# Opening loads, repeated weight rows and last PSUM tiles of a parallel attention and ReLU block

## Chip, cores and metric

The kernel runs on one core of a Trainium2 chip. Its time is device time in microseconds. Three runs of the kernel before gave 1164.60 to 1164.73, median 1164.63.

## The reference

```python
x: (1, 2048, 576); wqkv: (576, 1728); wo: (576, 576); w1: (576, 4608); w2: (4608, 576)   # all float32
xn  = layernorm(x)
# A: 32 heads of 18; each token attends to itself and to 7 earlier ones, 2 apart
q, k, v = heads(xn @ wqkv)
logits  = (q . k[pos - 2*w]) * 18 ** -0.5          # w = 0..7, masked where pos - 2*w < 0
a       = (softmax(logits) . v[pos - 2*w]) @ wo
# B: a dense block
b       = relu(xn @ w1) @ w2
return x + a + b
```

## The kernel before

The 2048 tokens are worked on in two phases (even and odd tokens) of 8 token tiles of 128 each; two token tiles make a block of 256 columns. Every matmul operand is split into a high part (rounded to fp32r) and a low part (the rest), and a product is the sum of high x high, low x high and high x low. 576 is four times 128 and 64 left over; the 64 remaining rows of a weight are kept twice, in the lower and the upper half of the 128 partitions, so that one matmul does two of the terms of the remainder.

The main loop runs over 288 steps `n` (phase, 12 chunks of 3 x 128 columns of w1, 4 blocks of tokens, 3 columns f). In a step TensorE does the 14 matmuls of `h_mm(n + 2)` (xn @ w1 into a PSUM tile `ph`), then the 12 of `o_mm(n)` (relu(h) @ w2 into PSUM tiles `po`, one for each of the two token tiles, accumulated over f). After f = 2, `o_out` adds the two `po` tiles to the token tiles in SBUF (VectorE, L606), which frees them for the next block. ScalarE takes ReLU of `ph` as `hhi` (L556), VectorE makes `hlo` (L559). `ph`, `po` and `pm` have two buffers each; a `po` takes two PSUM banks, a `ph` or `pm` one, so all eight banks are used. Attention, its projections (`qkv_tile`, `wo_a` to `wo_b`) and the next phase's normalisation are put between these steps at step numbers written in tables; VectorE's part of attention is dealt out by `run_bg` so that it keeps pace with TensorE.

Weights come through a list of tasks ordered by step. A task has a load into one of five staging tiles `st` and a split: `two()` makes the high part on ScalarE (L145) and the low part on VectorE (L149), or on GpSimd (L147) for a few steps. Loads are issued three tasks ahead of the splits by `stage_more`, all on SP's DMA queue, in order; each waits until its staging tile is free. `w1_task` loads a tile in one transfer for the 512 full rows and two for the 64 remaining ones (L157, L161, L162); `wo_tasks` loads five tiles, the fifth (kt = 4) being the 64 remaining rows, again in two transfers (L212, L213). The fifth wo tile is split at steps 119 and 263; f is 2 there.

The opening is written out by hand from L682 on. It loads the first two token tiles in halves on SP's and ACT's queue (`load_x`, L236), then w1 and w2 tiles and further token tiles on SP. The first tile is normalised by ScalarE, the second by VectorE, both are transposed by TensorE and split (`make_xt`), and then the first h matmuls start. At the end the last step adds the two halves of the columns of each token tile apart (L612) and stores them on both queues (L615, L617).

Of the kernel before, what the change touches and what calls it, by code (L numbers as in the profile page):

```python
# [10 lines left out]
F32 = mybir.dt.float32  # L11
F32R = mybir.dt.float32r
AF = mybir.ActivationFunctionType
# [4 lines left out]
P = 128  # L18
NPH = 2
NI = 8  # L20
# [5 lines left out]
C = 3  # L26
# [12 lines left out]
HEADW = (-9, -8, -7, -6, -5, -4)  # L39
# [16 lines left out]
def tile_body(ctx: ExitStack, tc: tile.TileContext, x, wqkv, wo, w1, w2, out):  # L56
    nc = tc.nc
    S, D = x.shape
# [5 lines left out]
    KT = 4  # L64
    DR = D - KT * P
    D2 = D // 2
    CUT = (slice(0, 256), slice(256, D))
# [22 lines left out]
    ps_o = pool("ps_o", 2, space=PSUM)  # L90
    ps_h = pool("ps_h", 2, space=PSUM)
    ps_m = pool("ps_m", 2, space=PSUM)
# [10 lines left out]
    for _ in range(WARM):  # L103
        nc.tensor.transpose(warm[:, 0, 0:P], ident, ident)

    x_v = x.rearrange("(p i two) d -> two i p d", i=NI, two=NPH)
    o_v = out.rearrange("(p i two) d -> two i p d", i=NI, two=NPH)


    t = {"pe": 0.0, "dve": 0.0}  # L110

    def mm(o, l, r, start, stop, n):
        nc.tensor.matmul(o, l, r, start=start, stop=stop)  # L113
        t["pe"] += n / 2400.0 + 0.002

    def dve(n):
        t["dve"] += (n + 130) / 960.0
# [6 lines left out]
    def split_task(step, load, split):  # L124
        tasks.append((step, load, split))

    def stage_more(ahead=AHEAD):
        while tasks and len(staged) < ahead:
            step, load, split = tasks.popleft()
            st = stp.tile([P, 640], F32, name="st")  # L130
            load(st)
            staged.append((step, split, st))
# [9 lines left out]
    step_now = None  # L142

    def two(hi, lo, src, n):
        nc.scalar.activation(hi, src, AF.Copy)  # L145
        if step_now in by_pool:
            nc.gpsimd.tensor_tensor(lo, src, f32(hi), op=ALU.subtract)  # L147
        else:
            nc.vector.tensor_tensor(lo, src, f32(hi), op=ALU.subtract)  # L149
            dve(n)  # L150

    W1, W2, WQ, WO = {}, {}, {}, {}

    def w1_task(step, key, f):
        def load(st):
            c = slice(f * P, (f + 1) * P)
            nc.sync.dma_start(  # L157
                st[:, 0:512].rearrange("p (k c) -> p k c", k=KT),
                w1[0 : KT * P, c].rearrange("(k p) c -> p k c", p=P),
            )  # L160
            nc.sync.dma_start(st[0:DR, 512:640], w1[KT * P : D, c])  # L161
            nc.sync.dma_start(st[DR:P, 512:640], w1[KT * P : D, c])  # L162

        def split(st):
            w = w1p.tile([P, 2, 5 * P], F32R, name="w1t")
            two(w[:, 0, :], w[:, 1, :], st[:, :], 640)
            W1[key] = w

        split_task(step, load, split)
# [36 lines left out]
    def wo_tasks(steps, key):  # L206
        def one(kt):
            def load(st):
                if kt < KT:
                    nc.sync.dma_start(st[:, 0:D], wo[kt * P : (kt + 1) * P, :])  # L210
                else:
                    nc.sync.dma_start(st[0:DR, 0:D], wo[KT * P : D, :])  # L212
                    nc.sync.dma_start(st[DR:P, 0:D], wo[KT * P : D, :])  # L213

            def split(st):
                if kt == 0:
                    a = wqp.tile([P, 7, D], F32R, name="wq")
                    b = vp.tile([P, 3, D], F32R, name="v")
                    WO[key] = [a[:, k, :] for k in range(7)] + [b[:, k, :] for k in range(3)]
                w = WO[key]  # L220
                two(w[kt], w[5 + kt], st[:, 0:D], D)

            return load, split

        for kt, step in enumerate(steps):
            split_task(step, *one(kt))


    X, XT, XN, MR = {}, {}, {}, {}

    def load_x(ph, i):
        X[ph, i] = xp.tile([P, D], F32, name="x")
        if ph == 0 and i < 2:
            for h, q in enumerate((nc.sync, nc.scalar)):
                c = slice(h * D2, (h + 1) * D2)
                q.dma_start(X[ph, i][:, c], x_v[ph, i][:, c])  # L236
            return
        nc.sync.dma_start(X[ph, i], x_v[ph, i])

    def stats(ph, i, parts=False, act=False):  # L240
        xt = X[ph, i]
# [283 lines left out]
    left = {(ph, i): 2 for ph in range(NPH) for i in range(NI)}  # L525

    def done(ph, i):
        left[ph, i] -= 1
        if left[ph, i] == 0:
            nc.sync.dma_start(o_v[ph, i], X[ph, i])  # L530


    slots = [(ph, c, tb, f) for ph in range(NPH) for c in range(NCH) for tb in range(NTB) for f in range(C)]
    H, PO = {}, {}
# [35 lines left out]
        h_out(n)  # L570

    def half(po, h):
        return po[:, 1, 0 : D - 256] if h else po[:, 0, 256:512]

    def o_mm(n, out=True, which=range(2)):
        ph, c, tb, f = slots[n]
        hi, lo = H[n]
        w = W2[ph, c, f]
        end = n == len(slots) - 1
        for k in which:  # L580
            if f == 0:
                PO[k] = ps_o.tile([P, 2, 512], F32, name="po")
            cs = slice(k * P, (k + 1) * P)
            terms = [(j, l, b, h) for j, (l, b) in enumerate(((hi, 0), (hi, 1), (lo, 0))) for h in range(2)]
            if end:
                terms.sort(key=lambda z: -z[3])
            for j, l, b, h in terms:
                mm(
                    half(PO[k], h), l[:, cs], w[:, b, CUT[h]],
                    f == 0 and j == 0, f == C - 1 and j == 2, D2,  # L590
                )
        if 1 in which:
            H.pop(n)
        if out:
            o_out(n, which)

    def o_out(n, which=range(2)):
        ph, c, tb, f = slots[n]
        if f < C - 1:
            return  # L600
        for k in which:
            i = 2 * tb + k
            acc = X[ph, i]
            if n < len(slots) - 1:
                whole = PO[k].rearrange("p b c -> p (b c)")[:, 256 : 256 + D]
                nc.vector.tensor_tensor(acc, whole, acc, op=ALU.add)  # L606
                dve(D)
                if c == NCH - 1:
                    done(ph, i)
                continue  # L610
            for h, c in reversed(list(enumerate(CUT))):
                nc.vector.tensor_tensor(acc[:, c], half(PO[k], h), acc[:, c], op=ALU.add)  # L612
                if h == 0 and i == NI - 1:
                    for q, p in (nc.sync, slice(0, P // 2)), (nc.scalar, slice(P // 2, P)):
                        q.dma_start(o_v[ph, i][p, c], acc[p, c])  # L615
                else:
                    (nc.scalar if h else nc.sync).dma_start(o_v[ph, i][:, c], acc[:, c])  # L617
            left[ph, i] -= 1
            assert left[ph, i] == 0


    todo = {}
# [10 lines left out]
    for ph in range(NPH):  # L633
        b = ph * SPP
        for c in range(NCH):
            for f in range(C):
                s = b + c * SPC + f
                first = ph == c == 0
                plan.append((HEADW[f] if first else s - 5, w1_task, ((ph, c, f), c * C + f)))
                plan.append((HEADW[3 + f] if first else s - 3, w2_task, ((ph, c, f), c * C + f)))  # L640
# [8 lines left out]
        for i in range(NI):  # L649
            z = s + WO_STEPS[i]  # L650
# [5 lines left out]
        if ph + 1 < NPH:  # L656
            e = b + SPP - SPC
            for i in range(NI):
                if i >= len(XT_STEPS):
                    z = e + 3 + 2 * i  # L660
                    at(z - 6, load_x, ph + 1, i)
                    late(z - 2, stats, ph + 1, i)
                    late(z - 1, norm, ph + 1, i)
                    at(z + 1, make_xt, ph + 1, i)
                    continue
                load, first, second, send, back, parts = (e + k for k in XT_STEPS[i])
                at(load, load_x, ph + 1, i)
                late(first, stats, ph + 1, i, False, True)
                late(second, norm_turned, ph + 1, i)
                late(send, xt_a, ph + 1, i)  # L670
                at(back, xt_f, ph + 1, i)
                at(parts, xt_s, ph + 1, i)
# [7 lines left out]
    by_pool.update((-9, -8, *range(UNIT0 - 5, UNIT0)))  # L680
    both, x_low, w_low, last = TERMS[0:4], TERMS[4:8], TERMS[9:13], [TERMS[8], TERMS[13]]
    load_x(0, 0)  # L682
    load_x(0, 1)
    nc.scalar.activation(spare, mhalf, AF.Exp)
    stage_more(1)
    load_x(0, 2)
    stage_more(4)
    load_x(0, 3)
# [40 lines left out]
    x2[1]()  # L729
    x2[3]()  # L730
    o_mm(0)
    o_mm(1)
    make_xt(0, 3, bank=ps_h)
    o_mm(2, out=False)
    stats(0, 4)
    s5 = stats(0, 5, parts=True)
# [6 lines left out]
    h4[0]()  # L743
    h4[1]()
    o_out(2, (0,))
    x4 = make_xt(0, 4, parts=True)
    for f in x4[:3]:
# [56 lines left out]
```

## Time and profile before

| | us |
|---|---|
| median of three runs | 1164.63 |
| the profiled execution | 1165.02 |
| its span, from first to last instruction | 1163.2 |
| TensorE busy (share of the span) | 1155.8 (99%) |
| VectorE busy | 822.1 (71%) |
| ScalarE busy | 308.7 (27%) |
| DMA, SP's queue, share of 16 engines | 25.1% |
| granted TensorE clock | 0.999 |

A row of the profile gives a line of the kernel, an engine, an operation, the tile written and the tiles read, and shapes. PE is TensorE, PEld its weight loads, DVE VectorE, ACT ScalarE, POOL GpSimd, SP the engine that issues most DMAs; a q behind a name is the engine's sequencer, where DMAs are issued. In a timeline the first number is the start and the second the length, both in us from the start of the span, and brackets give the idle time before and what ended it. In a chain of waits each row is what the next one waited for.

### The profile page before, as it was taken

Reading aid. Unit: us, or ns where it says so; the run is one execution under the profiler, and the core shown is the slowest. Engines: PE = TensorE matmul, PEld = TensorE weight load, DVE = VectorE, ACT = ScalarE, POOL = GpSimd, SP = SyncE. Lnnn points to the kernel's source line nnn. Section 1 sums busy time; section 2 is a strip of 40 time slices with the busy share of each in tenths; the row PEclk is TensorE's granted clock in tenths of the full one; section 3 lists DMA queues with packets and bytes.
Section 4 is the critical chain, followed back from the end, with each engine's and each line's share of the span. In section 5 each row is a group of like instructions: output and inputs, shape, how many; then the busy total and the mean of one; then the engine's idle time right before and its main releaser. Section 6 shows DMA issues by size and latency. Waiting matters only on the chain.

```text
span 1163.2 us, 21702 instructions
## 1 busy us (share of the span) xinstructions
PE 1155.8 (99%) x8916; PEld 1147.9 (99%) x8916; DVE 822.1 (71%) x1299; ACT 308.7 (27%) x748; POOL 44.8 (4%) x60
## 2 busy tenths in 40 slices
PE   8999999999999999999999999999999999999998
PEld 8999999999999999999999999999999999999998
DVE  7427885887687688876683288768768877887843
ACT  5312222131231221322433123222222312222310
POOL 3200100010000000000010001000100000000000
PEclk9999999999999999999999999999999999999999
DMA  5312211140331311364752113031312303113541
GB/s 184 98 34 77 70 47 54 39 112 1 94 81 30 89 34 44 96 163 106 184 159 70 42 53 96 21 81 40 85 36 59 110 1 101 50 31 91 125 99 62
DMA packets 150036, 88.66 MB, mean 76 GB/s; under 512 B 58560, under 2 KB 133824, under 8 KB 149936
## 3 DMA queue, kind: packets, MB, share of 16 engines
q1 hardware_dynamic: 146752, 78.38, 25.1%
q10 hardware_dynamic: 3184, 8.88, 2.6%
q8 instruction: 70, 1.15, 0.4%
q14 instruction: 30, 0.25, 0.1%
HBM read 67.90 MB, written 11.14 MB: 68 GB/s over the span
## 4 chain that ended last, share of the span: by engine, by line
PE 99%; DMA 0%; ACT 0%; DVE 0%; issue 0%; DVEq 0%; POOL 0%; ACTq 0%
PE ph L113 39%; PE po L113 39%; PE pm L113 20%; PE pm L286 0%; DMA x<-in_x 0%; DVE x L612 0%; PE pm L287 0%; DVE bst L250 0%; ACT xn L269 0%; ACT xn L270 0%; ACT xT L291 0%; PE po L286 0%; DVEq L800 0%; PE ph L287 0%; POOL nm L256 0%
## 5 line engine op out<-in xcount | busy, mean ns | idle before, releaser
L113 PE MATMUL ph<-xT,w1t 128*128 128x256 f32 x4018 | 505.1, 277 | 0.7 <-ACT xT L291 0.7
L113 PEld LDWEIGHTS ph<-xT,w1t 128*128 128x128 f32 x4018 | 487.0, 188 | 1.3 <-ACT xT L291 1.0
L113 PE MATMUL po<-w2t,hhi 128*128 128x256 f32 (+1 forms) x2304 | 395.3, 293 | 0.0
L113 PEld LDWEIGHTS po<-w2t,hhi 128*128 128x128 f32 x2304 | 337.3, 188 | 1.1
L556 ACT ACTIVATE hhi<-ph 128x256 fp32r<-128x256 f32 x287 | 109.9, 383 | 582.9 <-PE ph L113 570.5
L113 PE MATMUL po<-w2t,hlo 128*128 128x256 f32 (+1 forms) x1152 | 243.9, 292 | 0.0
L559 DVE SCALAR_TENSOR_TENSOR hlo<-ph,hhi 128x256 fp32r<-128x256 f32 x287 | 120.7, 421 | 165.0 <-ACT hhi L556 164.4
L113 PEld LDWEIGHTS po<-w2t,hlo 128*128 128x128 f32 x1152 | 190.1, 187 | 0.0
L113 PE MATMUL pm<-wq,xT 128*128 128x432 f32 x896 | 185.5, 358 | 0.0
L606 DVE TENSOR_TENSOR x<-po,x 128x576 f32<-128x576 f32 x190 | 143.0, 756 | 60.1 <-PE po L113 57.3
L113 PEld LDWEIGHTS pm<-wq,xT 128*128 128x128 f32 x896 | 163.8, 188 | 5.6
L421 DVE TENSOR_TENSOR pr<-qo,k 128x1152 f32<-128x1152 f32 x64 | 86.1, 1348 | 0.0
L424 DVE TENSOR_REDUCE lg<-pr 128x64 f32<-128x1152 f32 x64 | 85.1, 1343 | 0.0
L451 DVE TENSOR_TENSOR pr<-lg,v 128x1152 f32<-128x1152 f32 x64 | 84.7, 1349 | 0.0
L149 DVE TENSOR_TENSOR w2t<-st,w2t 128x576 fp32r<-128x576 f32 x72 | 55.8, 775 | 31.4 <-ACT w2t L145 31.4
L149 DVE TENSOR_TENSOR w1t<-st,w1t 128x640 fp32r<-128x640 f32 x70 | 58.8, 840 | 20.6 <-ACT w1t L145 20.5
L458 DVE TENSOR_TENSOR pr<-pr 128x288 f32<-128x288 f32 (+1 forms) x128 | 70.5, 600 | 0.0
L145 ACT ACTIVATE w2t<-st 128x576 fp32r<-128x576 f32 x72 | 49.3, 685 | 44.0 <-PE po L113 34.5
L390 ACT ACTIVATE k<-pm 128x144 f32<-128x144 f32 x64 | 18.7, 292 | 146.2 <-PE pm L113 146.2
L145 ACT ACTIVATE w1t<-st 128x640 fp32r<-128x640 f32 x72 | 52.8, 734 | 12.7 <-DMA st<-in_w 6.7
L427 POOL TENSOR_SCALAR_AFFINE_SELECT lg<-lg 1x512 f32<-1x512 f32 x8 | 9.9, 1232 | 810.0 <-DVE lg L424 810.0
L522 DVE TENSOR_TENSOR x<-pm,x 128x256 f32<-128x256 f32 (+1 forms) x32 | 13.1, 453 | 30.8 <-PE pm L113 30.8
(79 smaller groups left out, 461.8 us busy)
## 6 DMA issues: line engine op xcount, KB each, us to landing
st<-in_w SPq DMA_DIRECT2D x72, 288.0 KB, 3.2
st<-in_w SPq DMA_DIRECT2D x72, 256.0 KB, 3.2
st<-in_wqkv SPq DMA_DIRECT2D x32, 216.0 KB, 3.0
turned<-tr SPq DMA_DIRECT2D x64, 80.0 KB, 2.8
xn<-turned SPq DMA_DIRECT2D x16, 320.0 KB, 3.2
st<-in_w SPq DMA_DIRECT2D x144, 32.0 KB, 2.8
x<-in_x SPq DMA_DIRECT2D x14, 288.0 KB, 4.1
out<-x SPq DMA_DIRECT2D x14, 288.0 KB, 2.1
```

The source lines that it names most:

```text
L113: nc.tensor.matmul(o, l, r, start=start, stop=stop)
L145: nc.scalar.activation(hi, src, AF.Copy)
L149: nc.vector.tensor_tensor(lo, src, f32(hi), op=ALU.subtract)
L390: nc.scalar.activation(k[:, W - 1 + i, :], pq[:, 1, :], AF.Copy)
L421: nc.vector.tensor_tensor(pr[i], q, window(k, i), op=ALU.mult)
L424: nc.vector.tensor_reduce(lg[:, i], pr.pop(i).rearrange(heads, d=Dh), axis=AX.X, op=ALU.add)
L451: nc.vector.tensor_tensor(pr[i].rearrange(heads, d=Dh), e, window(v, i).rearrange(heads, d=Dh), op=ALU.mult)
L458: nc.vector.tensor_tensor(o, z[:, 0:n], z[:, n : 2 * n], op=ALU.add)
L522: nc.vector.tensor_tensor(acc, po[h], acc, op=ALU.add)
L556: nc.scalar.activation(hi, pt, AF.Relu)
L559: nc.vector.scalar_tensor_tensor(lo, pt, 0.0, f32(hi), op0=ALU.max, op1=ALU.subtract)
L606: nc.vector.tensor_tensor(acc, whole, acc, op=ALU.add)
```

## The change

Four edits. In the opening, the two halves of the first token tile both go on SP's queue, the second token tile goes whole on ACT's queue, the first w1 tile is asked for before it, and the remaining rows of that w1 tile go on ACT's queue. The high part of the first w1 tile is made by VectorE. The 64 remaining rows of each w1 tile and of wo come in one transfer, whose source has an outer dimension of 2 with step zero. In the last block, each of the two parts of the columns has a PSUM tile of its own, for both token tiles (`po` buffers for the first, `pm` for the second); the first token tile is stored whole.

```diff
     def two(hi, lo, src, n):
-        nc.scalar.activation(hi, src, AF.Copy)
+        if step_now == HEADW[0]:
+            nc.vector.tensor_copy(hi, src)
+        else:
+            nc.scalar.activation(hi, src, AF.Copy)
...
+    def twice(ap):
+
+        return bass.AP(ap.tensor, ap.offset, [[0, 2]] + [list(z) for z in ap.ap])
...
-            nc.sync.dma_start(st[0:DR, 512:640], w1[KT * P : D, c])
-            nc.sync.dma_start(st[DR:P, 512:640], w1[KT * P : D, c])
+            (nc.scalar if key == (0, 0, 0) else nc.sync).dma_start(st[:, 512:640], twice(w1[KT * P : D, c]))
...
-                    nc.sync.dma_start(st[0:DR, 0:D], wo[KT * P : D, :])
-                    nc.sync.dma_start(st[DR:P, 0:D], wo[KT * P : D, :])
+                    nc.sync.dma_start(st[:, 0:D], twice(wo[KT * P : D, :]))
...
-        if ph == 0 and i < 2:
-            for h, q in enumerate((nc.sync, nc.scalar)):
-                c = slice(h * D2, (h + 1) * D2)
-                q.dma_start(X[ph, i][:, c], x_v[ph, i][:, c])
+        if ph == i == 0:
+            for c in slice(0, D2), slice(D2, D):
+                nc.sync.dma_start(X[ph, i][:, c], x_v[ph, i][:, c])
             return
-        nc.sync.dma_start(X[ph, i], x_v[ph, i])
+        (nc.scalar if (ph, i) == (0, 1) else nc.sync).dma_start(X[ph, i], x_v[ph, i])
...
     def half(po, h):
+        if isinstance(po, list):
+            return po[h]
         return po[:, 1, 0 : D - 256] if h else po[:, 0, 256:512]
...
-            if f == 0:
+            if f == 0 and n == len(slots) - C:
+                if k:
+                    PO[k] = [ps_m.tile([P, c.stop - c.start], F32, name="pm") for c in CUT]
+                else:
+                    PO[k] = [ps_o.tile([P, 2, 512], F32, name="po")[:, 0, 0 : c.stop - c.start] for c in CUT]
+            elif f == 0:
                 PO[k] = ps_o.tile([P, 2, 512], F32, name="po")
...
-                if h == 0 and i == NI - 1:
-                    for q, p in (nc.sync, slice(0, P // 2)), (nc.scalar, slice(P // 2, P)):
-                        q.dma_start(o_v[ph, i][p, c], acc[p, c])
-                else:
+                if k:
                     (nc.scalar if h else nc.sync).dma_start(o_v[ph, i][:, c], acc[:, c])
-            left[ph, i] -= 1
-            assert left[ph, i] == 0
+            if k == 0:
+                done(ph, i)
...
     load_x(0, 0)
+    stage_more(1)
     load_x(0, 1)
     nc.scalar.activation(spare, mhalf, AF.Exp)
-    stage_more(1)
     load_x(0, 2)
```

## Prediction

> **What bounds the kernel now.** I read the page first: the busy shares and the chain of work that ended last.
>
> ```profile
> PE 1155.8 (99%) x8916; PEld 1147.9 (99%) x8916; DVE 822.1 (71%) x1299; ACT 308.7 (27%) x748; POOL 44.8 (4%) x60
> ...
> PE 99%; DMA 0%; ACT 0%; DVE 0%; issue 0%; DVEq 0%; POOL 0%; ACTq 0%
> ```
>
> TensorE is the bound from its first real matmul to its last. So only three things move the time: when that matmul starts, what follows the last one, and any hole made in between. The chain of waits, cut to the opening, gives the first:
>
> ```profile
> 0.73 2.92 DMA x<-in_x
> ...
> 3.67 0.83 DVE bst L250 x2
> ...
> 8.16 0.02 issue
> 8.19 0.61 ACT xT L291
> 8.79 0.04 issue
> 8.84 3.74 PE ph L113 x28
> ```
>
> The first token tile lands at 3.65, is normalised and transposed, and TensorE starts at 8.84, once the second tile's high part (8.19) is there too. The second tile's statistics start at 4.84 (timeline), its halves having been issued at 1.2 and landed within 3.4, by 4.6. Its normalised form is ready at 7.33 and TensorE takes it at 7.54, so it has 0.2 us of slack.
>
> The timeline of the end:
>
> ```profile
> 1158.27 1.60 DVE L612 TENSOR_TENSOR x<-po,x 128x320 f32<-128x320 f32 x4 [3.07 <-PE po L113]
> ...
> 1159.90 0.52 SPq L615 DMA_DIRECT2D out<-x  x1
> 1160.02 0.55 ACTq L615 DMA_DIRECT2D out<-x  x1
> ```
>
> VectorE's four additions begin only when all six matmuls of the first token tile are done (its 320-column part was complete at 1157.88), and the last store, issued at 1160.02, lands 2.2 later.
>
> Third, the place in the middle that the change reaches: the last 64 rows of wo.
>
> ```profile
> 479.51 0.69 ACT L145 ACTIVATE wq<-st 128x576 fp32r<-128x576 f32 x1 [0.50 <-DMA st<-in_wo]
> ...
> 480.23 0.76 DVE L149 TENSOR_TENSOR v<-st,wq 128x576 fp32r<-128x576 f32 x1 [0.19 <-ACT wq L145]
> 480.47 0.69 ACT L145 ACTIVATE w2t<-st 128x576 fp32r<-128x576 f32 x1 [0.28 <-DMA st<-in_w]
> ...
> 481.19 0.76 DVE L149 TENSOR_TENSOR w2t<-st,w2t 128x576 fp32r<-128x576 f32 x1 [0.20 <-ACT w2t L145]
> 481.77 0.38 ACT L556 ACTIVATE hhi<-ph 128x256 fp32r<-128x256 f32 x1 [0.62 <-PE ph L113]
> 482.19 0.42 DVE L559 SCALAR_TENSOR_TENSOR hlo<-ph,hhi 128x256 fp32r<-128x256 f32 x1 [0.24 <-ACT hhi L556]
> 482.55 1.54 DVE L606 TENSOR_TENSOR x<-po,x 128x576 f32<-128x576 f32 x2
> ```
>
> ScalarE stands waiting for that load (0.50 idle, released by the DMA). Behind it in VectorE's order are both low parts, hlo and, in this step, the two additions that free the PSUM tiles of `po`. TensorE wants these at 484.73:
>
> ```profile
> 484.73 0.68 PE L113 MATMUL po<-w2t,hhi 128*128 128x256 f32 x4
> ```
>
> The first addition ends at 483.3, so the slack is 1.4 us. The same stretch recurs 573.9 us later (ACT at 1053.35, additions at 1056.49).
>
> **The repeated rows: how many DMA engines carry them.** Before, the 64 remaining rows go in two transfers whose slowest dimension is 64. After, one transfer reads a source of 2 x 64 x 128 (for wo 2 x 64 x 576), the 2 with step zero. The trace shows how such a dimension is dealt: each transfer leaves sixteen completion marks. For all sixteen halo copies of 15 rows (L396) the first mark comes 1.25 to 1.46 us after the issue, too early for data, and the other fifteen from 2.63 on; the 112-row copies have their first at 3.0 or later. So 15 rows occupy 15 engines and the missing mark is given at once. I read this as whole outermost slices dealt to engines, which leaves two engines for an outermost 2. No row of before has so short a dimension, so the bounds are sixteen engines (cost nothing) and two; I take two, as the nearest row (15) follows the count. The Trainium skill, DMA: Bandwidth & Descriptors, section Rules for kernel authors, says that a leading zero-stride broadcast of c copies confines the whole DMA to at most c engines. The fifteen late marks agree with it; no run so far shows its case of 2. The same section advises one 128-partition transfer instead of two halves; by that alone the merging would save an issue of 0.59 us (L162) on SP, which nothing waits for.
>
> With two engines, a w1 remainder is 32.8 KB on each (4 KB before), a wo remainder 147.5 KB. Rate of one engine: the stretch 4.0 to 4.8 moved 317 GB/s with 512-byte rows, 19.8 per engine; the slices of 470.9 to 474.9 with 2304-byte rows peak at 415, so 26. I take 24 for wo and 22 for w1 beside x.
>
> **wo, twice.** A wo tile of 18.4 KB per engine lands in 2.8 (L210): 2.1 fixed plus 0.7. The remainder then lands 2.1 + 147.5/24 = 8.2 after its issue at 476.0 (freed by a DVE split, unchanged): 484.2 instead of 479.43. From there in VectorE's order: 0.08 + 0.72 (ACT start to DVE start, 479.51 to 480.23) + 0.76 + 0.76 + 0.42 + 0.76 = 3.5, so the first addition ends at 487.7, against 484.73: a hole of 3.0. The w2 tile queued behind it on the same two engines lands at 485.0 and is split by 485.8, just in time. Two occurrences: +6.0. At 26 GB/s a hole is 2.6, at 19.8 it is 4.3.
>
> **w1, 69 times in steady state: 0.** A remainder lands about 1.3 later (28.7 KB at 22). ScalarE waits for these loads eight times today, 1.7 at most; 3.0 then. The next `ph` tile is reused 4.8 us after its matmuls end and needs 0.8 of evacuation, which leaves 4.0; and the tiles loaded that tightly are split in steps without additions. Bounds 0 and +1.
>
> **Opening.** The remainder of the first w1 tile now goes first on ACT's queue, and the whole second token tile is behind it. On the two engines that is 32.8 + 18.4 = 51 KB on ACT's queue. SP's queue (first tile, w1, third tile) has more than that, so with equal shares 102 KB pass before the second tile is complete. In before about 40 KB per engine had passed by 4.1 (36.9 KB of x, landed at 4.58, some w1); the other 62 KB at 22 take 2.8, and with the 0.45 from last packet to landing it lands near 7.35. Its statistics start 2.5 later than 4.84; less the slack of 0.2, the first matmul is late by +2.3. If ACT's queue is favoured it lands at 5.9 (+0.9); at 19.8 GB/s and with the ramp of the first packets, +3.3. The first tile's second half, now queued behind its first on SP (issue 0.44 later) beside w1 packets, lands 0.2 to 0.7 later; that is covered by the second tile's delay, and is paid if that delay is gone. The second and third w1 remainders go over the same two engines: 153 KB until the second is complete, near 9.7, wanted at 8.71 + 2.3; the third near 11.9, wanted at 9.87 + 2.3: covered. The high part of the first w1 tile moves from ScalarE, where it hid before the transposes ended (6.63 to 7.35), to VectorE behind the second tile's normalisation. A one-input pass of 576 columns took 0.58 (L272), a two-input pass of 640 0.82; 0.3 to 0.8 here, beside the transposes and ScalarE's evacuation (7.33 to 8.79 before), so 0. GpSimd's low part (1.55) follows it; wanted 16 matmuls after the start, about 2.2 us: 0. The reordering on SP saves issues only.
>
> **Tail.** With a tile per part, the additions start when each part is done: 1157.9, 1158.3, 1158.7, and the last at 1159.1 after TensorE's end at 1159.02; it ends near 1159.5 instead of 1159.87. The first tile's store is one SP issue at 1158.8 (0.35 to 0.6), done before the last part's at 1159.55, which lands after 1.9 (L617), at 1161.5, or 1161.8 if the 590 KB of stores at 355 GB/s from 1159.75 on set it; before, 1162.2. I take -0.4 (-0.7 to 0). The second token tile's parts use `pm` tiles free since 1141.6, the first's use both `po` tiles, freed at 1153.5, wanted at 1154.05: no wait.
>
> **Sum.** 6.0 + 2.3 + 0 - 0.4 = +7.9 on the profiled execution's 1165.02 (span 1163.2 and 1.8 around it), so 1172.9. That execution is 0.4 above the median of the runs, 1164.63; forecast 1172.5. Its own range is 1168.5 to 1176.5.
>
> **Rivals.**
> *All sixteen engines carry the repeated rows* (dealt by destination rows). Then wo and w1 cost nothing, x of the opening competes for 0.0 to +0.5 and the tail gives -0.4: 1164.4, no slower than before. For it: the destination is 128 rows, as in every fast load here. Against: the 15-row marks. It decides at the wo remainder: if that lands within 5.2 us of its issue, there is no hole. Chance 0.17.
> *Two engines, but wo is hidden*: the load goes out before 473, or the additions don't end late. Then only +2.3 - 0.4: 1166.5. Against: SP issues it when its staging buffer is freed at 475.96, and nothing in the change frees that earlier. Chance 0.07.
> *Faster by more than 0.2%*: the tail and the opening's start together hold too little: 0.4, and 0.5 if x came earlier. Chance 0.02.
> The forecast keeps 0.74.
>
> **Numbers.** 0.2% is 2.3 us, about what a measurement of this kernel can tell from no change. The forecast is slower by more than that; the first rival and most of the second are within it: slower 0.75, same 0.23, faster 0.02. The range goes from 1164.0, to take in the first rival, to 1176.5.
>
> **What would show it.** Right: landing of the wo remainder near 8 us instead of 2.9; ScalarE's wait on `in_wo` 4 to 6 us, twice; TensorE idle about 3 near 485 and 1060, released by a VectorE addition; w1 remainders landing 1 to 2 later than the main part; second tile's statistics after 6, first `ph` matmul near 11; last addition ending 0.4 after TensorE. Wrong: wo remainder landing in 3, TensorE without holes, or a granted clock below 9 tenths after a hole, which I have not priced.

## The result, and the profile after

The changed kernel takes 1178.71 us (median of 5 runs, 1176.84 to 1180.75); the kernel before takes 1164.73 beside it. The ratio is 1.0122, 95% interval 1.0107 to 1.0137: 14.0 us slower. The forecast was 1172.5 with a range up to 1176.5, so the direction was right and the size was not. The runs of the changed kernel spread over 3.9 us where those of before spread over 0.3; their granted clocks go from 0.997 (the fastest) to 0.993 (the two slowest). The profiled execution took 1178.71 (span 1176.9, clock 0.994).

The page after, busy time and the chain that ended last:

```profile
PE 1161.3 (99%) x8916; PEld 1153.1 (98%) x8916; DVE 822.1 (70%) x1300; ACT 306.6 (26%) x747; POOL 44.8 (4%) x60
...
PE 96%; DMA 2%; DVE 1%; ACT 0%; issue 0%; POOL 0%; DVEq 0%
```

TensorE still does 8916 matmuls, but is busy 1161.3 instead of 1155.8. The same matmuls are busy 5.5 us longer, so this line alone says that idle time is not the whole loss. The chain, cut to the two places where wo's last rows arrive (start, us, what):

```profile
479.10 8.89 DMA st<-in_wo
...
488.01 0.62 ACT wq L148
...
491.30 2.48 PE po L113 x12
493.77 2.53 PE ph L113 x14
496.30 1.56 PE po L113 x12
497.86 1.59 PE ph L113 x14
```

```profile
1057.93 8.87 DMA st<-in_wo
...
1070.11 3.22 PE po L113 x12
1073.33 2.86 PE ph L113 x14
```

The transfer takes 8.9 us instead of 2.9 (the second of its two transfers before). Its completion marks in the trace are three: one 0.95 us after the issue and two late ones, at 8.72 and 8.89 (0.96, 8.57 and 8.87 in the second phase); by the prediction's reading of such marks, two engines carry it. TensorE then stands still for 3.30 and 3.28, released by VectorE's addition into x (timeline, the first matmuls behind each hole; in brackets the idle time):

```profile
491.30 0.78 PE L113 MATMUL po<-w2t,hhi 128*128 128x256 f32 x4 [3.30 <-DVE x L617]
...
1070.11 1.30 PE L113 MATMUL po<-w2t,hhi 128*128 128x256 f32 x4 [3.28 <-DVE x L617]
```

And the groups behind the hole, which take 1.56 and 1.59 everywhere else, take 2.48 and 2.53, and in the second phase 3.22 and 2.86. That is 1.86 and 2.93 more: a price that the prediction did not have.

The windows view shows what it is (stretch, length, busy time of PE, PEld, DVE, ACT and POOL, then the granted clock, DMA share and GB/s). The stretches are the periods at whose edges the granted clock changes, 3.413 us each:

```profile
4.12:7.53 3.41, 1.59 (x15) 1.35 (x14) 1.30 (x5) 1.55 (x2) 0.79 (x2) 1.00 1.00 327
7.53:10.94 3.41, 1.34 (x10) 0.80 (x9) 2.28 (x6) 1.13 (x3) 1.46 (x2) 1.00 0.53 140
10.94:14.36 3.42, 3.30 (x15) 3.30 (x16) 2.98 (x8) 1.83 (x5) 2.70 (x3) 0.50 0.96 322
...
488.81:492.22 3.41, 0.92 (x7) 0.95 (x8) 3.41 (x7) 1.10 (x3) 0.00 (x0) 1.00 0.44 118
492.22:495.64 3.42, 3.42 (x17) 3.42 (x17) 2.37 (x5) 0.00 (x0) 0.00 (x0) 0.50 0.05 16
1065.66:1069.08 3.42, 1.17 (x11) 0.97 (x9) 1.55 (x3) 1.83 (x4) 0.00 (x0) 1.00 0.36 108
1069.08:1072.49 3.41, 2.38 (x10) 2.41 (x11) 3.41 (x9) 0.00 (x0) 0.00 (x0) 0.50 0.36 114
1072.49:1075.90 3.41, 3.41 (x18) 3.41 (x17) 0.91 (x1) 0.00 (x0) 0.00 (x0) 0.50 0.00 0
```

After a period in which PE was busy for 0.92, 1.17 or 1.34 of 3.41 us the clock is 0.50 for the next one; after 1.59 it is not. In the second phase it stays at 0.50 for one period more (to 1075.90), and the first half-clock period still had 1.03 us of the hole in it (the last section compares such periods over all profiles). All edges fit one grid that runs on through the whole execution: 492.22 is 141 periods after 10.94, and 1069.08 is 310.

The opening in the timeline of VectorE and TensorE: the second token tile's statistics, and the first hidden-layer matmuls (start, us, ..., idle before and its releaser). The first row is of the kernel before, the others of the changed one:

```profile
4.84 0.81 DVE L250 BATCH_NORM_STATS2 bst<-x 128x6 f32<-128x288 f32 x2
...
7.05 0.82 DVE L254 BATCH_NORM_STATS2 bst<-x 128x6 f32<-128x288 f32 x2 [1.56 <-DMA x<-in_x]
...
11.06 4.99 PE L113 MATMUL ph<-xT,w1t 128*128 128x256 f32 x28 [0.69 <-ACT xT L295]
```

Statistics at 7.05 instead of 4.84, first matmul at 11.06 instead of 8.84, and the 28 take 4.99 instead of 3.74, beginning in the half-clock period shown above. Of the second tile's sixteen completion marks fourteen come by 5.86 and the last two at 6.96 and 7.03.

The sum over this execution: opening 2.22 + 1.25, first hole 3.30 + 1.86, second 3.28 + 2.93, the tail -0.5, together 14.3; 0.6 of it comes back in places not followed further (0.3 of the opening's 3.47 by 42 us, which leaves 3.2), and the span is 13.7 longer.

### The profile page after: what moved, and what is told of

It reads as the page before. It is cut to its first block, busy times and chain, and to the rows that moved or that the text cites. A ratio compares the mean times of both kernels' runs of the same rounds, so it can differ in the third digit from the quotient of the medians.

```text
span 1176.9 us, 21572 instructions
## 1 busy us (share of the span) xinstructions
PE 1161.3 (99%) x8916; PEld 1153.1 (98%) x8916; DVE 822.1 (70%) x1300; ACT 306.6 (26%) x747; POOL 44.8 (4%) x60
## 3 DMA queue, kind: packets, MB, share of 16 engines
q10 hardware_dynamic: 2946, 8.72, 2.5%
## 4 chain that ended last, share of the span: by engine, by line
PE 96%; DMA 2%; DVE 1%; ACT 0%; issue 0%; POOL 0%; DVEq 0%
PE ph L113 38%; PE po L113 37%; PE pm L113 20%; DMA st<-in_wo 2%; DMA st<-in_w 1%; PE pm L290 0%; DVE x L617 0%; DVE hlo L563 0%; DVE w2t L152 0%; DVE pr L462 0%; DVE v L152 0%; ACT wq L148 0%; DVE x L623 0%; ACT hhi L560 0%; PE pm L291 0%
## 5 line engine op out<-in xcount | busy, mean ns | idle before, releaser
L113 PE MATMUL po<-w2t,hhi 128*128 128x256 f32 x2292 | 394.6, 293 | 6.6 <-DVE x L617 6.6
L113 PE MATMUL po<-w2t,hlo 128*128 128x256 f32 x1146 | 243.1, 293 | 0.0
L113 PE MATMUL pm<-wq,oT 128*128 128x256 f32 x224 | 34.3, 292 | 0.0
```

## Experiments

All runs have the kernel before beside them on the same chip (medians 1164.63 to 1164.78). They were made in three groups, (a), then (b), then (c), and the expectations of the later ones rest on the earlier ones.

**1 (a). wo's remainder in two transfers again; all else as changed.**

```
-  nc.sync.dma_start(st[:, 0:D], twice(wo[KT * P : D, :]))
+  nc.sync.dma_start(st[0:DR, 0:D], wo[KT * P : D, :])
+  nc.sync.dma_start(st[DR:P, 0:D], wo[KT * P : D, :])
```

> The changed kernel with wo's remainder read again by two transfers of 64 rows; the w1 remainders, the opening and the tail stay changed. Theory (a transfer whose source counts two in its outermost dimension is moved by two DMA engines, and PE pays for its lateness twice, in idle time and then at half clock): the wo remainder lands 2.7 to 2.9 us after its issue instead of 8.9, ScalarE's wait for it, both PE holes of 3.3 and the half clock at 492 and 1069 us are gone; what is left is the opening's +3.2 and the tail's -0.5: 1164.7 + 2.7 = 1167.4. Rival (the holes come from the new order of the loads, not from this transfer): they stay, 1178.7.

Measured 1168.96 (1167.89 to 1169.36), ratio 1.0034 [1.0021, 1.0047]. Both holes are gone, and ScalarE's wait is back to 0.43:

```profile
482.38 0.69 ACT L148 ACTIVATE wq<-st 128x576 fp32r<-128x576 f32 x1 [0.43 <-DMA st<-in_wo]
```

So this one transfer costs 1178.71 - 1168.96 = 9.75 us, of which 6.6 are idle time. The rest of the loss, 4.2, is more than the 2.7 expected; runs 6 to 8 take it up.

**2 (a). One transfer of the same 147.5 KB, rows outermost, copies inside.**

```
-  nc.sync.dma_start(st[:, 0:D], twice(wo[KT * P : D, :]))
+  src = bass.AP(wo.tensor, wo[KT * P : D, :].offset, [[D, DR], [0, 2], [1, D]])
+  nc.sync.dma_start(st[:, 0:D], src)
```

> The changed kernel with wo's remainder still one transfer of repeated rows with the same 147.5 KB, but with the 64 rows as the outermost dimension and the two copies inside it (row, copy, column in place of copy, row, column); the rows of the remainder thus land interleaved, row 0 on partitions 0 and 1 and so on, so that the product with wo is not the reference's. Theory (the outermost count sets how many engines move it): it lands 2.7 to 3.2 us after issue, no PE hole, 1167.4. Rival (reading the same rows twice, or 147.5 KB in one transfer, is what is slow): 8.9 us and 1178.7.

One run: 1168.67, no hole. The load is issued at 480.2 and ScalarE's cast starts at 483.24 without waiting for it:

```profile
L219 SPq DMA_DIRECT2D st<-in_wo x2: 588/594/600, 480.2 to 1054.1; - x2
...
483.24 0.69 ACT L148 ACTIVATE wq<-st 128x576 fp32r<-128x576 f32 x1
```

(The first line is of the view of the tile in_wo, the second of ScalarE's timeline.) It has landed within 3.1 us, and its sixteen completion marks come 2.54 to 3.06 after the issue, none early. Same bytes, same rows read twice, same single transfer: only the order of the dimensions differs, and with it 5.8 us. Neither the zero step nor the size is what is slow.

**3 (c). No row repeated, but short outermost dimensions.** In the kernel before:

```
-  nc.sync.dma_start(st[0:DR, 0:D], wo[KT * P : D, :])
-  nc.sync.dma_start(st[DR:P, 0:D], wo[KT * P : D, :])
+  nc.sync.dma_start(st[0:DR, 0:D], every(wo[KT * P : D, :], 2))   # [[D, 2], [2 D, 32], [1, D]]
+  nc.sync.dma_start(st[DR:P, 0:D], every(wo[KT * P : D, :], 4))   # [[D, 4], [4 D, 16], [1, D]]
```

> The kernel before with wo's remainder in its two transfers of 64 rows, no row read twice by one transfer, but the rows of the first transfer in the order even, then odd (outermost count 2), those of the second in four groups, each of every fourth row (outermost count 4); the rows so land in another order and the product with wo is not the reference's. Theory (the outermost count of the source sets how many engines move a transfer): at 21.7 GB/s for an engine the first lands 2.1 + 73.7/21.7 = 5.5 and the second 2.1 + 36.9/21.7 = 3.8 us after its issue, against 2.7 to 2.9 before; PE's slack of 1.4 is passed by about 1: 1164.8 to 1167. Rival (a step of zero, the same rows read twice, is what is slow): both land within 3.0, 1164.8.

One run: 1172.38, slower than either theory said. The pair, issued at 475.84 and 476.55, holds ScalarE until 484.15:

```profile
484.15 0.69 ACT L145 ACTIVATE wq<-st 128x576 fp32r<-128x576 f32 x1 [5.30 <-DMA st<-in_wo]
```

That is 8.3 us after the first issue, with no zero step anywhere, so the rival falls. The number of late completion marks is again the outermost count: two for the first transfer, at 6.09 and 6.89 us, and four for the second, at 4.01, 4.66, 7.22 and 7.53, each with one mark at 1.0. My 5.5 and 3.8 were for each transfer alone. Two of the second's four marks come some 3 us behind the other two, which fits two engines shared with the first transfer. These would carry 32 + 16 rows = 110.6 KB, which at 21.7 GB/s gives an estimate of 2.1 + 5.1 = 7.2; that explains most of the miss.

**4 (a). TensorE kept at work in the holes.** The changed kernel with 26 matmuls into the next `ph` tile ahead of its group:

```
+  if n % SPP == UNIT0 + NU * UNIT_STEP + WO_AT - 3:
+      ph, c, tb, f = slots[m]
+      HP[m], HN[m] = ps_h.tile([P, TBN], F32, name="ph"), 0
+      for _ in range(26):
+          nc.tensor.matmul(HP[m], W1[ph, c, f][:, 0, 0:P], XT[ph, tb][:, 0, :], start=True, stop=True)
```

> The changed kernel with 26 extra matmuls (128x256, about 2.9 us) into the PSUM tile of the hidden layer ahead of the last ph group before each wo hole; the group that follows starts its accumulation anew. PE so has work in the time in which it stood still; the wo remainder still lands 8.9 us after issue, and the po group behind the hole still starts at 491.3 or very near. Theory (the clock gate halves the clock for windows of 3.41 us after the idle time): no granted clock of 0.5 at 492 and 1069, the po and ph groups behind the hole take 1.56 and 1.59 us again instead of 2.5 to 3.2: 1178.7 - 1.9 - 2.9 = 1173.9. Rival (the 4.8 us beside the idle time come from work of ScalarE and VectorE that queued up behind the late weights): stays 1178.7, whatever the clock; a second rival (the extra matmuls delay the following hidden layer): over 1179.

Measured 1175.81 (1174.17 to 1176.09), 2.9 less than the changed kernel although it does 52 matmuls more; the opening of its profiled execution happened to be 1.2 worse than that of the changed one (first matmul at 11.44, the 28 in 5.83). At the holes (chain):

```profile
1069.98 1.85 PE po L113 x12
1071.83 1.65 PE ph L113 x14
```

The weights are about as late as before (at the second hole 8.71 us after the issue, and the group starts at 1069.98, against 1070.11), but the groups take 1.85 and 1.65 instead of 3.22 and 2.86, and the granted clock stays 1.00 through both places (windows view of the second):

```profile
1067.83:1071.25 3.42, 3.23 (x27) 3.06 (x26) 3.42 (x8) 0.83 (x3) 0.00 (x0) 1.00 0.40 119
1071.25:1074.66 3.41, 3.41 (x30) 3.41 (x29) 2.74 (x6) 0.38 (x1) 0.00 (x0) 1.00 0.03 10
```

At the first hole they take 1.82 and 1.59. Both groups together thus take 3.41 and 3.50 behind the two holes, against 5.01 and 6.08 in the changed kernel and 3.15 where there is no wait: of the 4.8 us behind the holes 4.2 were clock, and the other 0.6 is the first group, which takes some 0.3 longer after any wait (run 5 has it too). The backlog of ScalarE and VectorE, the rival, is still there and leaves at most these 0.6.

**5 (c). Shorter holes.** No repeated rows but for the first 400 columns of wo's remainder in the first phase and 480 in the second:

```
+  e = 480 if key else 400
+  nc.sync.dma_start(st[:, 0:e], twice(wo[KT * P : D, 0:e]))
+  nc.sync.dma_start(st[0:DR, e:D], wo[KT * P : D, e:D])
+  nc.sync.dma_start(st[DR:P, e:D], wo[KT * P : D, e:D])
```

> The kernel without repeated rows and with the new opening, but with part of wo's remainder repeated in one transfer: its first 400 columns in the first phase, 480 in the second, the rest of the columns in two transfers. Theory: at 21.7 GB/s for an engine (147.5 KB in 8.9 - 2.1 us) the repeated parts land 2.1 + 102.4/21.7 = 6.8 and 2.1 + 122.9/21.7 = 7.8 us after issue, PE holes of 1.2 and 2.2; the first shows no half clock and costs 1.2, the second 2.2, or about 5 if it still lowers the clock: with the 1169.3 of the kernel without repeats 1172.7, to 1175.5. Rival (a hole costs 5 to 6 whatever its length): 1179 or more.

The median is 1175.44, but the four runs are 1172.75, 1174.84, 1176.04 and 1176.04, with clocks 0.999, 0.996, 0.996 and 0.996. The profiled one is the first: holes of 1.84 and 2.64, longer than the 1.2 and 2.2 expected, and no half clock behind either:

```profile
490.15 1.84 PE po L113 x12
...
1066.71 1.84 PE po L113 x12
```

The holes are longer because the theory priced the repeated part alone: in the first phase its last mark came 6.97 us after its issue (6.8 expected), but the small transfers behind it had fourteen marks by 2.35 us after the issue of the last one and the final two at 6.00 and 6.10, at 486.75, so they waited on the same two engines.

The hole of 2.64 lay across an edge of the grid: its two periods had PE busy 1.49 and 2.69 of 3.41. In run 3 a hole of 2.77 lay, all but its last 0.24, inside one period (0.88 busy) and cost a half-clock period, one of 2.92 lay across an edge (2.18 and 1.73 busy) and cost none. So whether a hole of this size is paid twice depends on where it falls in the grid. That fits the spread of the runs; in the three slower runs here only the mean clock was seen, not the place.

**6 (a), 7 (b). The opening without repeated rows of w1.** Run 6 is the changed kernel with all w1 remainders in two transfers, run 7 has wo's in two as well:

```
-  q.dma_start(st[:, 512:640], twice(w1[KT * P : D, c]))      # q: ScalarE's queue for the first tile, else SP's
+  q.dma_start(st[0:DR, 512:640], w1[KT * P : D, c])
+  q.dma_start(st[DR:P, 512:640], w1[KT * P : D, c])
```

> The changed kernel with every w1 remainder read by two transfers of 64 rows again (the first tile's on ScalarE's queue, where the change put it); wo's remainder stays one transfer of repeated rows. Theory: the second token tile, which stands behind the first w1 remainder on ScalarE's queue, lands near 5 instead of 7; first ph matmul near 9.0 to 9.4 instead of 11.06, no half clock before 15 us; both wo holes stay: 1164.7 + 5.15 + 6.2 - 0.5 = 1175.5, up to 1176.0. Rival (the opening is late because the second token tile now stands on one queue behind a weight load at all): first matmul stays near 11, 1178.7.

> The changed kernel without any transfer of repeated rows: w1's and wo's remainders in two transfers of 64 rows each; the opening's new order of loads, VectorE's cast and the tail stay. Theory now (the opening is late because the second token tile is read behind the first token tile's and a weight tile's transfers, and not because of the repeated rows): first ph matmul near 10.4 as in the run with w1's remainder in two, half the clock for one window behind it, no wo holes: 1164.7 + 1.6 + 1.4 - 0.5 = 1167.2. Rival (the prediction's: the repeated w1 remainder on two engines holds up the second token tile): first matmul at 9.4 or before, full clock, 1164.7 or less.

Run 6: 1178.08 (1177.30 to 1180.32). Run 7: 1169.28 (1169.20 to 1170.04), ratio 1.0040 [1.0027, 1.0054]. In neither did the opening come near what I expected at run 6 (first matmul at 9.0 to 9.4): it is at 10.44 in run 6 and at 12.09 in run 7, against 11.06 in the changed kernel. Run 7's second token tile and first matmuls:

```profile
7.83 0.82 DVE L257 BATCH_NORM_STATS2 bst<-x 128x6 f32<-128x288 f32 x2 [3.31 <-DMA x<-in_x]
...
12.09 6.01 PE L113 MATMUL ph<-xT,w1t 128*128 128x256 f32 x28 [0.69 <-ACT xT L298]
```

In the kernels with the new opening order the second tile's statistics start at 6.65 to 7.05 where w1's rows are repeated (the changed kernel and runs 1, 2 and 4) and at 6.44, 7.83, 6.93 and 7.11 where they are not (runs 6, 7, 8 and 5). So taking the repeated rows away does not cure the delay. They are not without effect: in the changed kernel the last two of the tile's sixteen marks come 1.1 us behind the others, as two loaded engines would have it. But in runs 6, 7, 8 and 5 the last mark is at 6.41, 7.80, 6.91 and 7.09 without them. That the new opening costs 1169.28 - 1164.31 (run 10) = 5.0, more than the 3.5 of the changed kernel's profile (2.22 + 1.25), goes with a later landing and a second half-clock period in run 7's profile.

**8 (b). Run 7 with 13 extra transposes on TensorE ahead of the first hidden-layer matmuls** (9 and 4, into the `ph` tile of the first group; in the engine's order they came behind the second tile's transposes).

> The kernel of the run before this one (no repeated rows) with 9 extra 128x128 transposes between the two token tiles' transposes and 4 more ahead of the first ph matmul, into the PSUM tile that this group then starts anew; TensorE's idle time of 1.3 and 0.7 us between 7.7 and 10.4 us is so filled. Theory (the opening pays for its idle time once more in half clock): first ph matmul still near 10.4 to 10.6, but its 28 take 3.7 instead of 4.9 to 5.2: 1.0 to 1.4 less than without them, 1165.9 to 1166.2. Rival (these 28 are slow because they wait for the low parts of the weights or tokens): the same time as without them, 1167.2.

Measured 1167.80 (1166.31 to 1170.15). In the profile the first matmul is later than in run 7 (13.01 for 12.09), although the second tile came earlier (statistics at 6.93 for 7.83), and still the 28 end at 16.45 instead of 18.10. The median is 1.5 less than run 7's, with ranges that overlap:

```profile
9.37:12.78 3.41, 3.30 (x16) 3.26 (x17) 2.36 (x6) 1.93 (x5) 2.17 (x2) 0.50 0.69 230
...
13.01 3.44 PE L113 MATMUL ph<-xT,w1t 128*128 128x256 f32 x28
```

The half-clock period (first row, windows view) is over when the 28 start, and they take 3.44; in run 7 the clock is 0.50 from 10.74 to 17.57, and they take 6.01. So they were slow by the clock, not by waiting for low parts.

**9 (c). Second token tile first on ScalarE's queue**, ahead of the w1 remainder; otherwise run 7.

```
   load_x(0, 0)
-  stage_more(1)
   load_x(0, 1)
+  stage_more(1)
```

> The kernel without repeated rows and with the new opening, but on ScalarE's queue the second token tile's load goes ahead of the first w1 tile's remainder, so that each of the two queues begins with one token tile. Theory (the second token tile is late because it is issued at 1.95 instead of by 1.2 us, behind which SP's w1 tile and third token tile take most of what the DMA engines move): issued at 0.73 it lands by 4.6 or before, its statistics start at 4.2 to 4.8, first ph matmul at 8.3 to 8.9, no half clock: 1163.8 to 1164.4, at or a little under the kernel before. Rival (the second tile is late because it comes in one transfer on one queue in place of two halves on both): statistics after 6, first matmul past 10, 1167 or more.

Measured 1164.82 (1164.63 to 1166.44) against 1164.63, ratio 1.0003 [0.9994, 1.0012].

```profile
5.54 0.81 DVE L257 BATCH_NORM_STATS2 bst<-x 128x6 f32<-128x288 f32 x2
...
9.54 3.74 PE L113 MATMUL ph<-xT,w1t 128*128 128x256 f32 x28 [0.69 <-ACT xT L298]
```

Swapping two issues takes 4.5 us off run 7: the second tile is back by 5.54, the first matmul comes at 9.54, and no half clock follows. What is left against 8.84 is 0.7, so the forecast of a start at 8.3 to 8.9 was too good; these 0.7 are now the first tile's, whose statistics start at 4.09 (3.67 before) and whose transposes start at 7.48 (6.78 before). It is the place in the queue, issued at 0.73 instead of 1.99, that delayed the second tile. Whether the w1 remainder ahead of it on ScalarE's queue did it, or the loads that SP had issued by then, is not told apart, and how the DMA engines shared their time between the two queues was not measured.

**10 (b). The tail alone**, in the kernel before (the part of the diff in the last two token tiles).

> The kernel before with the change of the last two token tiles alone (a PSUM tile for each part of the columns, additions as each part is done, one store for the first tile). Theory: the end comes 0.5 us after-for-after earlier, as in the trace of the changed kernel (3.67 from the end of TensorE to the end of the span instead of 4.18): 1164.2. Rival (the last stores' landing sets the end and the additions are hidden): 1164.7, no change.

Measured 1164.31 (1163.99 to 1164.64; 11 runs), ratio 0.9997 [0.9988, 1.0005]: 0.47 less, inside the interval of no change. Of all kernels here it is the fastest, but not by what can be told from no change.

**11 (b). w1's repeated rows, with the old opening order** and wo in two transfers.

> The kernel before with w1's remainders in one transfer of repeated rows, VectorE's cast of the first w1 tile and the tail as in the changed kernel; the order of the opening loads and wo's two transfers are the old ones. Theory now (the order of the loads, not the repeated rows, delays the opening): second token tile's statistics start at 4.8 as before, first ph matmul at 8.8 to 9.0, and w1's repeated rows cost nothing later: 1164.7 - 0.5 + 0 to 0.2 = 1164.3. Rival (the repeated w1 remainders on two engines are late for the first casts): first matmul at 10 or later, or a wait of TensorE inside the first groups, 1166 or more.

Measured 1166.58 (1166.08 to 1167.13), ratio 1.0016 [1.0007, 1.0025]. The second tile's statistics start at 4.70 and the first matmul at 8.69, as expected; but then TensorE waits for the second w1 tile:

```profile
11.06 2.63 PE L113 MATMUL ph<-xT,w1t 128*128 128x256 f32 x20 [0.91 <-ACT w1t L148]
```

ScalarE's cast of it stood 1.64 for the load and ran at 10.28 (8.71 before). TensorE ends at 1160.52 instead of 1159.02, and this difference is there by the hundredth matmul and grows no more: so the repeated rows of w1 do cost some 1.5 us in the opening. In the changed kernel they are hidden, because everything there is later still: run 1 with them takes 1168.96, run 7 without them 1169.28.

## Why the prediction was wrong, point by point

**What failed: every gap was priced as idle time at full clock.** The sum was 6.0 + 2.3 - 0.4 = 7.9. The groups behind the gaps took 1.25 + 1.86 + 2.93 = 6.0 longer, and 7.9 + 6.0 = 13.9 is near the 14.0 measured (the idle terms came to 8.3, and 0.6 came back elsewhere). Run 4 shows that 4.2 of the 4.8 at the holes is the clock, and run 8 that the opening's share is the clock too. The prediction named a clock below 9 tenths after a hole as what would make it wrong and left it out of sum and range; the trace of before shows the half clock only in its last 2 us, where no matmul is left. The Trainium skill, TensorE: Matmul & The Clock Gate, Part 1: The HAM clock gate, has a free-running window of 3413 ns and a clock of half or full by the activity in it; both agree with the edges and the 0.50 above. The Trainium skill warns there of idle gaps over about 3.4 us. Here the measurement decides otherwise: holes of 3.30 and 3.28 us halved the clock, and behind the second one 2.25 us of idle time inside one period was enough.

**Two engines for an outermost two: right.** The transfer left two late completion marks, run 2 shows it with the same bytes, run 3 without a repeated row, and the rival of sixteen engines falls. The landing was 8.89 and 8.87, 8.2 forecast: (8.89 - 2.1) for 147.5 KB is 21.7 GB/s for an engine, not 24. The rule of the Trainium skill that the prediction set beside it (DMA: Bandwidth & Descriptors, Rules for kernel authors) also wants a dimension whose size is a multiple of 16 outermost, and run 2, with 64 rows outermost, agrees.

**The holes' idle time: nearly right**, 3.30 and 3.28 for 3.0, in part because two errors offset each other: the load landed 0.7 later than forecast, and from there to the end of the addition it took 3.2 (487.99 to 491.16) instead of 3.5. The order behind the late load was as described (both low parts, hlo, the addition, then `po`).

**w1 in steady state: right.** ScalarE's longest wait on these loads is 2.7 (3.0 forecast), and no PE hole comes from it.

**The opening: right number, and by luck.** The second tile landed at 7.03 for 7.35 and the start moved by 2.22 for 2.3. I put it down to the repeated remainder on two engines. Two late marks are there, but they account for 1.1 us, and runs 6 and 7 are about as late without the repeated rows; run 9 shows that the place in the queues decides. The equal shares for the two queues, from which the 7.35 came, were assumed, and no run here shows them. The step "second and third w1 remainders: covered" holds only under that delay (run 11).

**The tail: right in size**, 0.5 for 0.4 in the profile, 0.47 in run 10. Its additions start when each part is done, the last ending at 1173.74 after TensorE's end at 1173.23. In runs 1 and 11 the profiled span shows none of that gain: the last store is issued 0.54 after TensorE's end as in run 10, but its last mark comes 2.7 us after that issue instead of 2.1; why is open.

**The rivals.** wo was not hidden: its load went out at 479.10, 3.1 later than before, as everything did by the opening.

## What to carry to other kernels

When one engine is the bound, price a gap in its work twice: once as idle time, and once as what the next few microseconds cost if the clock drops; look at the windows of the granted clock, not at the idle time alone. In a transfer, put the long dimension outermost and copies inside: the same rows and bytes took at most 3.1 us instead of 8.9. And in an opening look at the place of a load in its queue: swapping two issues was worth 4.5 us.

## What the runs showed of the hardware

- The clock halves by the busy time of a fixed period of 3.413 us, not by the length of a gap. Over all profiles, periods at full clock with PE busy up to 1.42 us were followed by half clock, and with 1.59 or more they were not; between these both were seen (1.49, twice, and 1.53 followed by half clock, another 1.49 not).
- Getting back to full clock asks for more: half-clock periods with PE busy 2.38 to 2.73 were followed by another one, those with 3.03 or more by full clock. So a gap that reaches into a half-clock period can cost a second one: 1.03 us of it did in the changed kernel, 0.24 in run 3 did not.
- A source whose outermost dimension counts two leaves two late completion marks, one that counts four leaves four (run 3), and the same bytes with 64 outermost leave sixteen, 2.54 to 3.06 us after the issue (run 2).
- Transfers of few engines hold up what is queued behind them: the pair of run 3 took 8.3 us together, where 5.5 and 3.8 were estimated for each alone (neither was run alone), and the small transfers of run 5 had fourteen of sixteen marks by 2.35 us and the last two at 6.00 and 6.10.
